# Weights of the second layer converted during the first and kept in DRAM; the exponent moved by two ScalarE passes

## The chip, the cores and the metric

One core of a Trainium2 chip. The metric is the device time of one launch in microseconds, taken as the median over runs. Engines are called by the profile's names: PE (TensorE), DVE (VectorE), ACT (ScalarE), POOL (GpSimd), SP (the queue that issues nearly all DMAs here).

## What is computed

```python
X = np.fft.fft(np.fft.fft(x, axis=1), axis=2)      # x: (2, 3008, 256)
t = X.real.astype(np.float32).reshape(6016, 256)
h = t @ moe_w_in                                   # 256 -> 2048
g = np.where(h >= 1, h, np.where(h <= -1, 0.0, (h + 1) ** 2 / 4))
y = g @ moe_w_out                                  # 2048 -> 256
h = y @ moe2_w_in
return (np.maximum(0.01 * h, h) @ moe2_w_out).astype(np.float32)
```

The four weight matrices are float64, everything else is float32.

## The kernel before

The tokens are cut into eight units of 752, and the 2048 hidden features into sixteen slices of 128. One **step** n is one unit and one slice: 128 steps for the first layer (N1 = 128), 128 for the second, then four more to empty the pipe. The loop over the steps is at line 674. A matrix product keeps nearly float32 precision by splitting each operand into a high part and a low part and adding three products (high·high, high·low, low·high).

**A first-layer step** (`layer_1`, line 624) on PE is `first_1` (6 matmuls into a PSUM pair `p`, of which there are two) and `second` for step n − 4 (12 matmuls into `acc`). In between, DVE makes `aa` (line 635), the two halves of `h` (638, 639) and the maximum (648, for step n − 1); ACT makes two clamped halves (641, 645), the high part `gh` (569, for step n − 2) and a square (652); POOL makes the low part `gl` (573, for step n − 2), which `second` reads two steps later. **A second-layer step** (`layer_2`, line 655) has 24 matmuls, and less work elsewhere: ACT 660 and 569, DVE 661, POOL 573. Each sixteenth step ends with `store` (575), two copies on ACT and two on DVE.

**Weights** arrive as float64 in chunks of 128 x 512 (`w1`, `w2` for the first layer, `w3`, `w4` for the second, eight chunks each), 512 KB a chunk, into a ring of four buffers `rw`. `ToF32` (line 200) turns a chunk into float32 with integer operations on the two 32-bit halves of a float64:

- `begin`: the sign is taken off the high word, by ACT (`Abs`, line 215) or, while `clamping[0]` is set (all first-layer steps), by DVE (line 212);
- `exponent`: DVE clamps (line 219), then shifts and masks (line 221);
- `join`: DVE puts back the sign (line 225) and the last three bits of the mantissa (line 228).

After that a chunk is split into a high part (ACT: 248 or 263) and a low part (DVE: 252 or 267; for `w2` POOL at 267).

**The order of the work** is the program's own: each engine runs its instructions in the order in which they are issued here. Up to the first step, a list (`ORDER`, line 135) gives it; the eight `w1` chunks and `w2` chunks 0 to 3 are converted there. From then on a table `jobs` gives the functions to call at the end of a step. `plan` (599) puts the seven stages of a chunk on seven steps in a row. `w2` chunk j, 4 to 7, starts at step 1 + 3(j − 4), so that its `begin`, `exponent` and `join` fall on steps 3, 4, 5 for the first and 12, 13, 14 for the last. `w3` starts at step 114 and `w4` at step 126 (lines 612 to 617): `plan_late` (603) puts `exponent` and `join` on one step, and the two splits on the next. `split_y` (591) splits the first layer's result of one unit and half: ACT 593, DVE 594; for unit 0 at steps 118 and 121.

Of the kernel before, what the change touches and what calls it, by code (L numbers as in the profile page):

```python
# [9 lines left out]

F32 = mybir.dt.float32
FR = mybir.dt.float32r
I32 = mybir.dt.int32
I64 = mybir.dt.int64
AF = mybir.ActivationFunctionType
ALU = mybir.AluOpType

B, S, D, DFF = 2, 3008, 256, 2048
P = 128
# [107 lines left out]

LEAST = float(np.array(896 << 20, np.uint32).view(np.float32))  # L130
MOST = float(np.array((1151 << 20) - 1, np.uint32).view(np.float32))

ORDER = [s.strip() for s in """
load_w1 1, load_w1 4, load_x 0 0, load_cd, load_x 0 1, load_w1 2, load_x 0 2, w1_begin 1, load_w1 3,
w1_exponent 1, w1_begin 4, w1_join 1, w1_exponent 4, add_x 0 0, load_w1 0, g_product 1, load_me 2, w1_join 4,
# [24 lines left out]
def fnet_moe_kernel(ctx: ExitStack, tc: tile.TileContext, xpq, dft_e, dft_o, dft_d, sgn,  # L162
                    w1, w2, w3, w4, out):
    nc = tc.nc
    PSUM = bass.MemoryType.PSUM

    def pool(n, bufs, stack=ctx, side="left"):
        return stack.enter_context(tc.tile_pool(name=n, bufs=bufs, side=side, reuse_waits="tile"))
# [20 lines left out]
    V, A, G, T = nc.vector, nc.scalar, nc.gpsimd, nc.tensor  # L189
    g128 = sm.tile([P, NF], F32, name="g128")  # L190

    clamping = [False]

    def load_w(w, j):

        t = rw.tile([P, 512], I64, tag="rw", name="rw")
        nc.sync.dma_start(out=t, in_=w[j])
        return t

    class ToF32:  # L200

        def load(self, w, j):
            self.raw = load_w(w, j)

        def begin(self):
            v = self.raw.bitcast(I32).rearrange("p (n w) -> p n w", w=2)
            self.low, self.high = v[:, :, 0], v[:, :, 1]
            self.tmp = cv.tile([P, 512], I32, tag="tw", name="tw")  # L210
            if clamping[0]:
                V.tensor_scalar(out=self.tmp, in0=self.high, scalar1=0x7FFFFFFF, scalar2=None,  # L212
                                op0=ALU.bitwise_and)
            else:
                A.activation(self.tmp.bitcast(F32), self.high.bitcast(F32), AF.Abs)

        def exponent(self):
            t = self.tmp
            V.tensor_scalar(out=t.bitcast(F32), in0=t.bitcast(F32), scalar1=LEAST, scalar2=MOST,  # L219
                            op0=ALU.max, op1=ALU.min)  # L220
            V.tensor_scalar(out=t, in0=t, scalar1=3, scalar2=0x3FFFFFF8,  # L221
                            op0=ALU.logical_shift_left, op1=ALU.bitwise_and)

        def join(self):
            V.scalar_tensor_tensor(out=self.tmp, in0=self.high, scalar=-0x40000000, in1=self.tmp,  # L225
                                   op0=ALU.bitwise_and, op1=ALU.bitwise_or)
            c = cv.tile([P, 512], I32, tag="cw", name="cw")
            V.scalar_tensor_tensor(out=c, in0=self.low, scalar=29, in1=self.tmp,  # L228
                                   op0=ALU.logical_shift_right, op1=ALU.bitwise_or)
            self.f32 = c.bitcast(F32)  # L230

    def new_wa(j, nm):
        return wp.tile([P, 2, 4, P], FR, tag="wa", name=f"{nm}{j}")

    def first_weights(j):

        c = ToF32()
        t = {}

        def views():  # L240
            v = t["w"].rearrange("p q (h e) f -> p q h e f", e=2)
            s = c.f32.rearrange("p (q h f) -> p q h f", q=2, h=2)
            return [(v[:, q, :, 0, :], v[:, q, :, 1, :], s[:, q]) for q in range(2)]

        def high():
            t["w"] = new_wa(j, "wc")
            for hi, _, s in views():
                A.copy(hi, s)

        def low():  # L250
            for hi, lo, s in views():
                V.tensor_tensor(out=lo, in0=s, in1=hi.bitcast(F32), op=ALU.subtract)
            wa[j] = t["w"]

        return [lambda: c.load(w3, j), lambda: None, c.begin, c.exponent, c.join, high, low]

    def second_weights(w, j, nm, engine):
        c = ToF32()
        t = {}

        def high():
            t["w"] = wpb.tile([P, 2, 2, D], FR, tag="wb", name=f"{nm}{j}")
            A.copy(t["w"][:, :, 0, :], c.f32.rearrange("p (q d) -> p q d", q=2))

        def low():
            v = t["w"]
            engine.tensor_tensor(out=v[:, :, 1, :], in0=c.f32.rearrange("p (q d) -> p q d", q=2),  # L267
                                 in1=v[:, :, 0, :].bitcast(F32), op=ALU.subtract)
            wb[j] = v

        return [lambda: c.load(w, j), lambda: None, c.begin, c.exponent, c.join, high, low]

    with tc.manual_schedule():
# [256 lines left out]
        N1 = NU * NF  # L530
# [60 lines left out]
        def split_y(u, d):  # L591
            y = yp[u % 2].tile([P, 2, 2, H4], FR, tag="yh", name=f"yh{u}{d}")
            A.copy(y[:, 0], yt[u][:, d])
            V.tensor_tensor(out=y[:, 1], in0=yt[u][:, d], in1=y[:, 0].bitcast(F32), op=ALU.subtract)
            yh.setdefault(u, {})[d] = y

        jobs = {}

        def plan(step, stages, at=0):
            for i, s in enumerate(stages[at:]):  # L600
                jobs.setdefault(step + i, []).append(s)

        def plan_late(step, st):

            load, _, begin, exponent, join, high, low = st
            plan(step, [load, lambda: None, begin, lambda: (exponent(), join()), lambda: (high(), low())])

        for j in range(4, 8):
            plan(1 + 3 * (j - 4), w2s[j])
        w3s = [first_weights(j) for j in range(8)]  # L610
        w4s = [second_weights(w4, j, "wd", V) for j in range(8)]
        for j in range(8):
            if j < 3:
                plan(N1 - 14 + 3 * j, w3s[j])
            else:
                plan_late(N1 - 4 + 3 * (j - 3), w3s[j])
            plan_late(N1 - 2 + 2 * j, w4s[j])
        for d in range(2):
            plan(N1 - 10 + 3 * d, [lambda d=d: split_y(0, d)])
        for u in range(1, NU):  # L620
            plan(N1 + NF * (u - 1) + 8, [lambda u=u: split_y(u, 0)])
            plan(N1 + NF * (u - 1) + 11, [lambda u=u: split_y(u, 1)])
# [1 line left out]
        def layer_1(n):  # L624

            new = n < N1
            if new:  # L630
                u, f = divmod(n, NF)
                w, o = (378, 1) if u % 4 == 0 else (H4, 0)
                p = first_1(u, f)
                aa = ta.tile([P, 378], F32, tag="aa", name="aa")
                V.scalar_tensor_tensor(out=aa[:, :w], in0=ct[u][:, :w], scalar=g128[:, f:f + 1],  # L635
                                       in1=p[:, 0, :w], op0=ALU.mult, op1=ALU.add)
                hp[n] = h = th.tile([P, 2, H4], F32, tag="h", name="h")
                V.tensor_tensor(out=h[:, 0], in0=aa[:, 0:H4], in1=p[:, 1, 0:H4], op=ALU.subtract)  # L638
                V.tensor_tensor(out=h[:, 1], in0=aa[:, o:o + H4], in1=p[:, 1, o:o + H4], op=ALU.add)  # L639
                rp[n] = r = t5.tile([P, 2, H4], F32, tag="r", name="r")  # L640
                A.activation(r[:, 0], h[:, 0], CLAMP, scale=15.5)  # L641
            if 0 <= n - 2 < N1:
                high(n - 2)
            if new:
                A.activation(r[:, 1], h[:, 1], CLAMP, scale=15.5)  # L645
            if 0 <= n - 1 < N1:
                gp[n - 1] = g = rp.pop(n - 1)
                V.tensor_tensor(out=g, in0=hp.pop(n - 1), in1=g, op=ALU.max)  # L648
            if 0 <= n - 2 < N1:
                low(n - 2)  # L650
            if new:
                A.activation(r, r, AF.Square, scale=0.5 / 15.5, bias=0.5)  # L652
                sums(n)
# [18 lines left out]
                    store(m, m < N1)  # L672

        for n in range(2 * N1 + LAG):
            clamping[0] = n < N1
            if n < N1:
                layer_1(n)
            else:
                if n < N1 + 2:
                    layer_1(n)  # L680
                if n == N1 + 1:
                    only1.close()
                    right.close()
# [53 lines left out]
```

## Time and profile before

| | us |
|---|---|
| median of 3 runs | 1064.48 (1064.13 to 1065.47) |
| the profiled execution, its own time | 1063.04 |
| its span, first to last instruction | 1061.3 |
| PE busy | 1013.8 (96%) |
| DVE busy | 643.9 (61%) |
| ACT busy | 603.1 (57%) |
| POOL busy | 489.0 (46%) |

Busy times are sums over a program whose stages differ: the transform and the first weights up to about 90 us, the first layer's steps to about 510, the second layer's after that. PE's busy share is an upper bound, since its matmuls overlap. A row of the timeline gives start, duration, engine, line, operation and tiles, then in brackets how long the engine sat idle before it and what released it.

### The profile page before, as it was taken

How to read it: one execution, taken by the hardware profiler on the slowest of the kernel's cores; microseconds unless marked ns; L12 is line 12 of the kernel's file. 1: busy time of each engine (PE TensorE's matmuls, PEld its weight loads, DVE VectorE, ACT ScalarE, POOL GpSimd, SP SyncE). 2: the span in 40 equal slices, each digit the busy share in tenths (PEclk: the TensorE clock that was granted, in tenths of full speed). 3: DMA queues.
4: the chain of work that ended last, by engine and by line, in shares of the span. 5: the costliest groups of instructions: out<-in, count | busy, mean ns of one | idle time of the engine just before them, and what ended most of it. 6: DMA issues, size and time to landing. Idle time of an engine off the chain costs nothing.

```text
span 1061.3 us, 14375 instructions
## 1 busy us (share of the span) xinstructions
PE 1013.8 (96%) x5656; PEld 977.8 (92%) x5656; DVE 643.9 (61%) x952; ACT 603.1 (57%) x934; POOL 489.0 (46%) x274
## 2 busy tenths in 40 slices
PE   7996779999999999997898999999999999999998
PEld 6656779999999999997897999999999999999998
DVE  5988998878787878799999523232322323223221
ACT  2347568888888888875764444444444444444433
POOL 1014565656555655544443444444444444444443
PEclk9898999999999999999999999999999999999999
DMA  9921110000000000000131000000000000000000
GB/s 299 337 64 40 40 40 2 1 1 1 1 1 1 1 1 2 1 21 23 58 99 41 30 1 1 30 1 30 1 1 30 1 30 1 1 30 1 30 1 30
DMA packets 9859, 35.04 MB, mean 33 GB/s; under 512 B 1216, under 2 KB 1216, under 8 KB 9536
## 3 DMA queue, kind: packets, MB, share of 16 engines
q1 hardware_dynamic: 8928, 30.98, 8.0%
q0 software_dynamic: 864, 3.15, 1.6%
q8 instruction: 44, 0.72, 0.3%
q14 instruction: 23, 0.19, 0.1%
HBM read 27.96 MB, written 6.16 MB: 32 GB/s over the span
## 4 chain that ended last, share of the span: by engine, by line
PE 77%; DVE 15%; DMA 3%; issue 2%; ACT 2%; POOL 0%; SPq 0%; DVEq 0%; POOLq 0%; ACTq 0%
PE acc L564 43%; PE q L551 23%; PE p L540 10%; DVE cw L228 2%; DVE r L648 2%; DMA rw<-in_w_dram 2%; DVE tw L221 2%; DVE tw L219 1%; DVE tw L225 1%; DVE aa L635 1%; DVE h L639 1%; DMA x<-in_xpq_dram 1%; DVE h L638 1%; DVE s L661 1%; DVE tw L212 1%
## 5 line engine op out<-in xcount | busy, mean ns | idle before, releaser
L573 POOL TENSOR_TENSOR gl<-s,gh 128x752 fp32r<-128x752 f32 x128 | 234.3, 1830 | 297.7 <-ACT gh L569 297.7
L573 POOL TENSOR_TENSOR gl<-r,gh 128x752 fp32r<-128x752 f32 x128 | 236.8, 1850 | 195.6 <-ACT gh L569 171.9
L661 DVE TENSOR_TENSOR s<-q,s 128x752 f32<-128x752 f32 x128 | 120.2, 939 | 298.3 <-ACT s L660 298.3
L551 PE MATMUL q<-yh,wc 128*128 128x376 f32 x1536 | 287.6, 336 | 8.6 <-DVE s L661 8.6
L564 PE MATMUL acc<-gh,wb 128*128 128x376 f32 x1024 | 283.5, 338 | 1.6 <-POOL wb L267 1.3
L564 PE MATMUL acc<-gh,wd 128*128 128x376 f32 x1024 | 278.6, 333 | 0.0
L551 PEld LDWEIGHTS q<-yh,wc 128*128 128x128 f32 x1536 | 267.3, 190 | 10.8 <-DVE s L661 7.2
L569 ACT CAST gh<-s 128x752 fp32r<-128x752 f32 x128 | 105.1, 821 | 161.2 <-PE acc L564 152.3
L564 PEld LDWEIGHTS acc<-gh,wb 128*128 128x128 f32 x1024 | 188.5, 190 | 5.0 <-ACT r L645 2.3
L564 PE MATMUL acc<-gl,wb 128*128 128x376 f32 x512 | 173.6, 339 | 16.8 <-POOL gl L573 16.7
L564 PEld LDWEIGHTS acc<-gh,wd 128*128 128x128 f32 x1024 | 186.1, 188 | 0.1
L660 ACT ACTIVATE s<-q 128x752 f32<-128x752 f32 x128 | 102.2, 799 | 126.1 <-PE q L551 126.0
L564 PE MATMUL acc<-gl,wd 128*128 128x376 f32 x512 | 170.5, 333 | 0.0
L540 PE MATMUL p<-bt,wa 127*128 127x376 f32 (+3 forms) x768 | 156.8, 340 | 9.3 <-DVE h L639 6.1
L540 PEld LDWEIGHTS p<-bt,wa 128*128 128x128 f32 (+1 forms) x768 | 136.2, 191 | 13.0 <-issue 4.7
L648 DVE TENSOR_TENSOR r<-h,r 128x752 f32<-128x752 f32 x128 | 122.7, 958 | 3.5 <-ACT r L652 3.5
L641 ACT ACTIVATE r<-h 128x376 f32<-128x376 f32 x128 | 66.4, 519 | 97.5 <-DVE h L638 86.6
L564 PEld LDWEIGHTS acc<-gl,wb 128*128 128x128 f32 x512 | 97.4, 190 | 21.8 <-POOL gl L573 21.8
L635 DVE SCALAR_TENSOR_TENSOR aa<-ct,g,p 128x376 f32<-128x376 f32 (+1 forms) x128 | 77.3, 604 | 56.7 <-PE p L540 56.6
L652 ACT ACTIVATE r<-r 128x752 f32<-128x752 f32 x128 | 106.8, 834 | 4.1
L569 ACT CAST gh<-r 128x752 fp32r<-128x752 f32 x128 | 103.2, 806 | 0.2 <-DVE r L648 0.2
L564 PEld LDWEIGHTS acc<-gl,wd 128*128 128x128 f32 x512 | 96.1, 188 | 0.0
(71 smaller groups left out, 661.0 us busy)
## 6 DMA issues: line engine op xcount, KB each, us to landing
rw<-in_w_dram SPq DMA_DIRECT2D x32, 512.0 KB, 3.5
out_dram<-o SPq DMA_DIRECT2D x16, 376.0 KB, 2.4
x<-in_xpq_dram SPq DMA_DIRECT2D x6, 512.0 KB, 6.7
x<-in_xpq_dram POOLq DMA_DIRECT2D x6, 512.0 KB, 7.5
me<-in_dft_e_dram SPq DMA_DIRECT2D x4, 567.0 KB, 16.6
mo<-in_dft_o_dram SPq DMA_DIRECT2D x2, 1128.0 KB, 20.3
cd<-in_dft_d_dram SPq DMA_DIRECT2D x1, 256.0 KB, 6.1
sg<-in_sgn_dram SPq DMA_DIRECT2D x1, 1.0 KB, 6.2
```

Of the source, the lines that this page charges most:

```text
L221: V.tensor_scalar(out=t, in0=t, scalar1=3, scalar2=0x3FFFFFF8, op0=ALU.logical_shift_left, op1=ALU.bitwise_and)
L540: T.matmul(p[:, j, :n], lhsT=w[:m, 2 * j + x, :], rhs=b[:m, 2 * j + y, :n], start=(a == 0), stop=(a == 2))
L551: T.matmul(p[:, t, :H4], lhsT=w[:, 2 * d + x, :], rhs=y[d][:, z, t, :], start=(a == 0), stop=(a == 5))
L564: T.matmul(acc[k][:, :H4], lhsT=w[:, x, m * P:(m + 1) * P], rhs=y[:, t, :], start=(f == 0 and i == 0), stop=(f == NF - 1 and i == 2))
L569: A.copy(gh[n], gp[n])
L573: G.tensor_tensor(out=gl[n], in0=gp.pop(n), in1=gh[n].bitcast(F32), op=ALU.subtract)
L635: V.scalar_tensor_tensor(out=aa[:, :w], in0=ct[u][:, :w], scalar=g128[:, f:f + 1], in1=p[:, 0, :w], op0=ALU.mult, op1=ALU.add)
L641: A.activation(r[:, 0], h[:, 0], CLAMP, scale=15.5)
L648: V.tensor_tensor(out=g, in0=hp.pop(n - 1), in1=g, op=ALU.max)
L652: A.activation(r, r, AF.Square, scale=0.5 / 15.5, bias=0.5)
L660: A.activation(g, p, AF.Copy, scale=0.01)
L661: V.tensor_tensor(out=g, in0=p, in1=g, op=ALU.max)
```

## The change

- **Conversion** (`ToF32`): `begin` is now two ACT passes, everywhere: one multiplies the high word, read as float32, by 2^-9 and holds it within ±240, the other multiplies by 2^-103 in place. Together they lower the exponent by 112. The DVE clamp and the DVE way of taking off the sign are gone; `exponent` is one DVE pass, and `join` is cut into `sign` and `rest`.
- **`w3`**: chunk j is loaded at step 20 + 12j, `begin` comes 2 steps later, `exponent` 3, `sign` 6, and `rest` 9, with a DMA that writes the float32 chunk (256 KB) to a DRAM scratch. At step 122 + 2j it is read back into an `rw` buffer, and three steps later split into `wc`.
- **`w4`**: loaded at step 125 + 2j, `begin` and `exponent` 2 steps later, `join` 3, both splits 4.
- **`split_y`** of unit 0 moves from steps 118 and 121 to 102 and 108.

```diff
+from concourse.act_funcs import IDENTITY_SAT240 as HOLD
...
+    sp = ctx.enter_context(tc.tile_pool(name="sp", bufs=1, space=bass.MemoryType.DRAM))
...
-            if clamping[0]:
-                V.tensor_scalar(out=self.tmp, in0=self.high, scalar1=0x7FFFFFFF, scalar2=None,
-                                op0=ALU.bitwise_and)
-            else:
-                A.activation(self.tmp.bitcast(F32), self.high.bitcast(F32), AF.Abs)
+            t = self.tmp.bitcast(F32)
+            A.activation(t, self.high.bitcast(F32), HOLD, scale=2.0 ** -9)
+            A.activation(t, t, AF.Copy, scale=2.0 ** -103)
...
-            V.tensor_scalar(out=t.bitcast(F32), in0=t.bitcast(F32), scalar1=LEAST, scalar2=MOST,
-                            op0=ALU.max, op1=ALU.min)
-            V.tensor_scalar(out=t, in0=t, scalar1=3, scalar2=0x3FFFFFF8,
+            V.tensor_scalar(out=self.tmp, in0=self.tmp, scalar1=3, scalar2=0x7FFFFFF8,
                             op0=ALU.logical_shift_left, op1=ALU.bitwise_and)
...
+        def spill():
+            c.rest()
+            t["dram"] = sp.tile([P, 512], F32, name=f"w3f{j}")
+            nc.sync.dma_start(out=t["dram"], in_=c.f32)
+
+        def load():
+            t["f32"] = rw.tile([P, 512], I64, tag="rw", name="rf").bitcast(F32)[:, :512]
+            nc.sync.dma_start(out=t["f32"], in_=t["dram"])
...
-        return [lambda: c.load(w3, j), lambda: None, c.begin, c.exponent, c.join, high, low]
+        return [lambda: c.load(w3, j), c.begin, c.exponent, c.sign, spill, load, high, low]
...
-            if j < 3:
-                plan(N1 - 14 + 3 * j, w3s[j])
-            else:
-                plan_late(N1 - 4 + 3 * (j - 3), w3s[j])
-            plan_late(N1 - 2 + 2 * j, w4s[j])
+            plan_at(20 + 12 * j, *zip((0, 2, 3, 6, 9), w3s[j]))
+            plan_at(N1 - 6 + 2 * j, *zip((0, 3, 3), w3s[j][5:]))
+            plan_at(N1 - 3 + 2 * j, *zip((0, 1, 2, 2, 3, 4, 4), w4s[j]))
         for d in range(2):
-            plan(N1 - 10 + 3 * d, [lambda d=d: split_y(0, d)])
+            plan_at(N1 - 26 + 6 * d, (0, lambda d=d: split_y(0, d)))
...
-            clamping[0] = n < N1
```

`plan_at(step, (offset, stage), ...)` puts each stage on the step at its offset.

## Rows read from the trace of the kernel before

**Rows 1.** Part 1 of the page: busy time, share of the span, instructions.

```profile
PE 1013.8 (96%) x5656; PEld 977.8 (92%) x5656; DVE 643.9 (61%) x952; ACT 603.1 (57%) x934; POOL 489.0 (46%) x274
```

**Rows 2.** Busy time by stretch: PE, PEld, DVE, ACT, POOL; then clock, DMA, GB/s.

```profile
100.00:120.00 20.00, 16.06 (x89) 14.84 (x88) 19.69 (x25) 10.83 (x18) 10.61 (x6) 1.00 0.08 26
...
300.00:400.00 100.00, 99.90 (x578) 99.02 (x577) 80.41 (x133) 80.94 (x134) 58.31 (x32) 1.00 0.00 1
...
700.00:800.00 100.00, 100.00 (x585) 100.00 (x584) 29.08 (x29) 42.33 (x54) 44.19 (x25) 1.00 0.02 9
```

**Rows 3.** Timeline of a first-layer step without conversion, around 301 to 308.

```profile
301.39 0.61 DVE L635 SCALAR_TENSOR_TENSOR aa<-ct,g,p 128x378 f32<-128x378 f32 x1 [0.61 <-PE p L540]
...
302.95 0.93 DVE L648 TENSOR_TENSOR r<-h,r 128x752 f32<-128x752 f32 x1
...
303.09 0.81 ACT L569 CAST gh<-r 128x752 fp32r<-128x752 f32 x1
...
304.03 1.81 POOL L573 TENSOR_TENSOR gl<-r,gh 128x752 fp32r<-128x752 f32 x1 [1.29 <-ACT gh L569]
...
304.35 0.84 ACT L652 ACTIVATE r<-r 128x752 f32<-128x752 f32 x1
...
307.56 0.33 PE L564 MATMUL acc<-gl,wb 128*128 128x376 f32 x1
```

**Rows 4.** Timeline of steps 3 to 15, where `w2` chunks 4 to 7 are converted.

```profile
92.18 0.60 DVE L635 SCALAR_TENSOR_TENSOR aa<-ct,g,p 128x378 f32<-128x378 f32 x1
...
94.84 2.02 DVE L212 TENSOR_SCALAR tw<-rw 128x512 int32<-128x512 int32 x1
...
99.18 0.42 DVE L219 TENSOR_SCALAR tw<-tw 128x512 f32<-128x512 f32 x1
99.63 1.92 DVE L221 TENSOR_SCALAR tw<-tw 128x512 int32<-128x512 int32 x1
...
103.88 0.69 DVE L225 SCALAR_TENSOR_TENSOR tw<-rw,tw 128x512 int32<-128x512 int32 x1
...
104.11 2.10 POOL L573 TENSOR_TENSOR gl<-r,gh 128x752 fp32r<-128x752 f32 x1 [2.84 <-ACT gh L569]
...
104.67 2.09 DVE L228 SCALAR_TENSOR_TENSOR cw<-rw,tw 128x512 int32<-128x512 int32 x1
...
145.01 0.60 DVE L635 SCALAR_TENSOR_TENSOR aa<-ct,g,p 128x378 f32<-128x378 f32 x1
```

**Rows 5.** PE's timeline from step 117 to step 144, across the change of layer.

```profile
462.93 1.19 PE L540 MATMUL p<-bt,wa 128*128 128x376 f32 x6
...
504.52 1.30 PE L540 MATMUL p<-bt,wa 128*128 128x376 f32 x6
...
509.31 2.22 PE L551 MATMUL q<-yh,wc 128*128 128x376 f32 x12
...
578.55 3.91 PE L551 MATMUL q<-yh,wc 128*128 128x376 f32 x12 [2.94 <-DVE s L661]
...
588.46 2.21 PE L551 MATMUL q<-yh,wc 128*128 128x376 f32 x12
```

**Rows 6.** ACT's groups by line and shape: count, busy us, mean ns, idle before.

```profile
L215 ACT ACTIVATE tw<-rw 128x512 f32<-128x512 f32 x24 | 15.9, 674 | 13.4 <-DMA rw<-in_w_dram 13.2
L248 ACT CAST wc<-cw 128x256 fp32r<-128x256 f32 x16 | 5.7, 401 | 6.3 <-DVE cw L228 6.3
...
L263 ACT CAST wd<-cw 128x512 fp32r<-128x512 f32 x8 | 4.9, 618 | 3.9 <-DVE cw L228 3.8
```

**Rows 7.** ACT's timeline: two `begin` passes, and two of the three table loads.

```profile
66.93 1.50 ACT L215 ACTIVATE tw<-rw 128x512 f32<-128x512 f32 x2
...
85.80 1.28 ACT L641 ACT_TABLE_LOAD   x1
...
515.80 1.28 ACT L215 ACT_TABLE_LOAD   x1
```

**Rows 8.** DMA issues: count, KB each, median us from issue to landing.

```profile
rw<-in_w_dram SPq DMA_DIRECT2D x32, 512.0 KB, 3.5
```

More of the change, by code (lines that the diff above doesn't have):

```diff
@@ L126, in _token_rows @@
     return np.concatenate(rows)
-LEAST = float(np.array(896 << 20, np.uint32).view(np.float32))
-MOST = float(np.array((1151 << 20) - 1, np.uint32).view(np.float32))
 ORDER = [s.strip() for s in """
@@ L190, in fnet_moe_kernel @@
     g128 = sm.tile([P, NF], F32, name="g128")
-    clamping = [False]
     def load_w(w, j):
@@ L210, in begin, with sign, rest @@
             self.tmp = cv.tile([P, 512], I32, tag="tw", name="tw")
-            if clamping[0]:
-                V.tensor_scalar(out=self.tmp, in0=self.high, scalar1=0x7FFFFFFF, scalar2=None,
-                                op0=ALU.bitwise_and)
-            else:
-                A.activation(self.tmp.bitcast(F32), self.high.bitcast(F32), AF.Abs)
+            t = self.tmp.bitcast(F32)
+            A.activation(t, self.high.bitcast(F32), HOLD, scale=2.0 ** -9)
+            A.activation(t, t, AF.Copy, scale=2.0 ** -103)
         def exponent(self):
-            t = self.tmp
-            V.tensor_scalar(out=t.bitcast(F32), in0=t.bitcast(F32), scalar1=LEAST, scalar2=MOST,
-                            op0=ALU.max, op1=ALU.min)
-            V.tensor_scalar(out=t, in0=t, scalar1=3, scalar2=0x3FFFFFF8,
+            V.tensor_scalar(out=self.tmp, in0=self.tmp, scalar1=3, scalar2=0x7FFFFFF8,
                             op0=ALU.logical_shift_left, op1=ALU.bitwise_and)
-        def join(self):
-            V.scalar_tensor_tensor(out=self.tmp, in0=self.high, scalar=-0x40000000, in1=self.tmp,
+        def sign(self):
+            V.scalar_tensor_tensor(out=self.tmp, in0=self.high, scalar=-0x80000000, in1=self.tmp,
                                    op0=ALU.bitwise_and, op1=ALU.bitwise_or)
+        def rest(self):
             c = cv.tile([P, 512], I32, tag="cw", name="cw")
@@ L230, in join @@
             self.f32 = c.bitcast(F32)
+        def join(self):
+            self.sign()
+            self.rest()
     def new_wa(j, nm):
@@ L238, in first_weights @@
         t = {}
+        def spill():
[5 more added lines that the diff above has]
+            nc.sync.dma_start(out=t["f32"], in_=t["dram"])
         def views():
             v = t["w"].rearrange("p q (h e) f -> p q h e f", e=2)
-            s = c.f32.rearrange("p (q h f) -> p q h f", q=2, h=2)
+            s = t["f32"].rearrange("p (q h f) -> p q h f", q=2, h=2)
             return [(v[:, q, :, 0, :], v[:, q, :, 1, :], s[:, q]) for q in range(2)]
@@ L601, in plan, with plan_at @@
                 jobs.setdefault(step + i, []).append(s)
-        def plan_late(step, st):
-            load, _, begin, exponent, join, high, low = st
-            plan(step, [load, lambda: None, begin, lambda: (exponent(), join()), lambda: (high(), low())])
+        def plan_at(step, *stages):
+            for at, s in stages:
+                jobs.setdefault(step + at, []).append(s)
         for j in range(4, 8):
```

## The prediction

> **What bounds the kernel now.** I read the busy shares first: PE is busy for 96% of the span, DVE for 61% [rows 1]. That average says little, so the second view is the busy time by stretch [rows 2]. From 300 to 400 us PE is full: 578 matmuls in 100 us, 18 a step, so a first-layer step takes 3.11 us. From 700 to 800 it is full too: 585 matmuls, 24 a step, 4.10 us. From 100 to 120 PE is busy for 16.06 of 20 us, and DVE for 19.69: there DVE sets the pace. PE's timeline shows a second such stretch. It starts steps 117 and 128 at 462.93 and 509.31, 46.4 us for eleven steps that cost 34.2 at 3.11 us; steps 128 and 144 start at 509.31 and 588.46, 79.2 us for sixteen that cost 65.6 [rows 5]. That is 12.2 + 13.6 = **25.8 us lost around the change of layer**. In the first stretch DVE starts steps 3 and 15 at 92.18 and 145.01, 52.8 us for twelve that cost 37.3 [rows 4]: **15.5 us lost early**. Both are the stretches with weight conversion; the rest of the steps runs at PE's pace.
>
> Third, the timeline of one step, to see how much room there is. Without conversion DVE idles 0.61 us a step before `aa`, waiting for PE [rows 3]. `gl`, the last link of a step's chain, starts at 304.03 and takes 1.81; PE wants it at 307.56 [rows 3]. So the chain has **1.7 us of slack**: something that delays DVE or ACT once by less costs nothing, and some 0.6 us a step is won back.
>
> Last, why conversion is so dear for DVE. `L219` takes 0.42, and `L221` behind it 1.92; `L225` takes 0.69, and the like-sized `L228` behind it 2.09 [rows 4]. POOL's `gl` (104.11, 2.10) stands between [rows 4]: the first pass behind `L648` gets through, the second is held until POOL is done. A held pass costs about 1.4 us more, and each step has one POOL instruction to be held by.
>
> **Part 1, the early stretch.** Per chunk the change takes away `L212` (2.02 at the first chunk, which was held; taken as 0.42, like `L219`, for three more) and puts one pass in the place of `L219` and `L221` [rows 4]. The one that stays is first behind `L648`, so it costs what `L219` does, 0.42, and not 2.3: 1.9 saved. `join` stays at 0.69 + 2.09. Sum: 4 x 1.9 + 2.0 + 3 x 0.4 = 10.8 us, **taken as 11**. ACT gets two passes a chunk, each bounded by 0.67 [rows 6]; in three steps it has 3 x 2.5 us of its own (80.94 us in 100 [rows 2]), plus 1.35 and one split of 0.62 [rows 6], 9.5 us. DVE needs (52.8 - 10.8)/4 = 10.5. So ACT hides the passes; if DVE got faster than that, ACT would be next. The lower bound is 8, if the single `exponent` pass is held at half of the chunks (4 x 1.4 / 2 = 2.8 less). The upper is 15.5, all of the loss, should `rest` no longer be held because ACT, and so `gl`, runs later.
>
> The Trainium skill speaks against moving a multiplication this way: ScalarE: Activation LUTs, section "Rules for kernel authors", gives mul, max and min to VectorE, as the faster engine per element. The rows bear the rule out for one pass alone (0.67 on ACT, 0.42 on DVE). By it the four chunks would lose 0.25 us a pass, and this term would be near -2 in place of 11; but the pass that goes was a held one, and on the engine that is full.
>
> **Part 2, the change of layer.** `w3`'s conversion leaves it altogether: per `w3` chunk DVE keeps only the low split, per `w4` chunk it loses the clamp. For the second layer's steps count two at a time, one chunk of each kind, against 8.2 us of PE. DVE's own work is 29.08/24.4 = 1.2 us a step [rows 2], 2.4. `exponent` 0.42, `sign` and `rest` 0.69 each [rows 4], the low splits of `w4` and `w3` (two inputs, 512 elements a row each, so `L225`'s 0.69 each) make 3.2. That is 5.6 without holds, and 8.4 with one hold of 1.4 a step. The same count for before has five chunks in six steps, each 0.42 + 0.42 + 3 x 0.69 = 2.9: 14.5 + 7.2 + 6 x 1.4 = 30.1 us, where the rows give 79.2 x 6/16 = 29.7, so the count can be trusted. After, it gives 0 to 0.2 us lost per two steps, 0 to 2 for sixteen steps. ACT has (42.33/24.4) x 2 = 3.5 of its own [rows 2], plus 1.35 + 0.62 + 0.80 [rows 6] = 6.3 of 8.2: hidden.
>
> Two new waits stand in DVE's queue: `exponent` of `w4` is issued on the step of its own `begin`, and both low splits on that of their high splits, so DVE stands still until ACT gets there, with the next step's `aa` or `L661` behind it, and PE behind that. At step 125 this can be priced: `L648` ends at 303.9, ACT's square at 305.2, then a high split of 0.40 [rows 3, 6]; POOL holds until 305.84; the two lows end near 306.6, where `aa` should have started at 304.5. That is 2.1 late against 1.7 of slack: 0.4 lost. At step 127 ACT's two passes and a further split come on top, but PE then has the second layer's first twelve matmuls, which need neither; taken as 0.5, bound 3. In the second layer `p` or `q` has two buffers, and DVE frees one well ahead. **Sum: 25.8 - 1.8 = 24 us**, bounds 19 (the waits cost all of 3, the holds 4) and 25.8.
>
> The reloads: SP issues 16 more DMAs (8 writes, 8 reads, 256 KB), and the DMA engines have nothing else then. 512 KB land in 3.5 us [rows 8]; a reload has three steps, over 9 us, less the time it waits for an `rw` buffer, freed a step before. Hidden. If it came later than about 8 us, ACT would stop in front of its high split, and `gh` of the step behind it.
>
> **Part 3, the steady first layer** gets what has left: per `w3` chunk two ACT passes on one step (1.35 against some 0.6 of idle time: 0.75 late, within the slack), and three DVE passes on three steps, 0.42, 0.69, 0.69 against 0.61 each [rows 3, 4], all first behind `L648`; POOL's `gl` is then held for up to 0.6, within the slack. The write stands in SP's queue behind `rest`, with only the next load behind it, three steps later. That is nothing per chunk while each delay stays below 1.7. The two `split_y` (steps 102, 108) are different: DVE waits for ACT's copy, as at step 125, about 2.1 late: 0.4 each. **Cost taken as 1 us**; from 0 to 3.
>
> **Part 4, before the first step.** Twelve chunks get one more ACT pass (at most 0.67) and one DVE pass less (0.42); in a chain of one chunk this is 0.25 longer, on a busy DVE 0.42 shorter. The last place where it counts is 66.93, two `begin`s together [rows 7]: the chain to 85.80 gets about 0.5 longer there. Table loads: `Abs` and the clamp of line 641 need a load between them in both directions (85.80 and 515.80, 1.28 each [rows 7]), the copies and squares none. The load at 515.80 goes, which lies in the stretch counted in part 2. That at 85.80 is on the chain; no row tells if HOLD's table has the clamp. **Taken as 0**, from 1.5 gained (load gone) to 1.5 lost.
>
> **The sum.** 11 + 24 - 1 + 0 = 34 us. Against the profiled execution's own 1063.0 that is 1029.0; the median of the runs is 1.4 above it, so 1030.
>
> **The rivals.**
> - *The waits for ACT keep DVE the bound in the change of layer* (chance 0.12). One more hold and 0.4 of waiting for every two steps, 10.2 against 8.2, so 2.0 x 8 = 16 less part 2's allowance of 2: 14 lost. For: both waits are new, and the count with holds already fills 8.2. Against: one POOL instruction a step can hold only once. 1044.
> - *The spread work is not free* (0.10). If each `w3` chunk loses one hold beyond slack, 8 x 1.4 = 11: 1041. For: DVE and ACT are 80% busy there [rows 2]. Against: every DVE pass stands first.
> - *HOLD and the clamp are in different tables* (0.04). Two loads of 1.28 for each of twelve chunks. Early, ACT's 9.5 becomes 12.1 in three steps against DVE's 10.5, 4 x 1.6 = 6 lost; in the middle 1.35 + 2.56 is 3.3 late, 1.6 over the slack, x 8 = 13. 1049. The Trainium skill's page ScalarE activation tables: per-element evaluation and per-set limits, section "What a function is on this engine", puts functions of different sets one load of 1283 ns apart; the rows' 1.28 agrees.
> - *Slower* (0.05): nothing of a chunk's work fits the first layer. Held at every pass, a chunk costs 0.42 + 2 x 0.69 + 3 x 1.4 = 6.0 us of DVE; if PE lost all of it, 8 x 6.0 = 48 in place of 1: 1077. It decides from 35/8 = 4.4 us a chunk. Against: 0.61 us of idle time in each of twelve steps, 7.3 us a chunk.
>
> **How the numbers follow.** The forecast has 0.67, the four rivals 0.31, no change 0.02. Its own bounds are 1063.0 + 1.4 less (15.5 + 25.8 - 0 + 1.5 = 42.8) and less (8 + 19 - 3 - 1.5 = 22.5): 1022 to 1042. The range goes up to 1044, which takes in the first two rivals. A measurement here can tell about 0.2% (2 us) from no change. Faster 0.93, same 0.02, slower 0.05.
>
> **What would show it.** Right: from 100 to 150 us PE at 90% or more, where it was 80%; from 460 to 590 PE with no waits for DVE over 1 us; from 160 to 450 the same step of 3.11; two table loads; `L661` in the second layer with idle time before it from the start. Wrong: a gap of PE at each `w3` chunk, twelve steps apart; loads in pairs; ACT waiting for the reload.

## The result, and the profile after

| | before | after |
|---|---|---|
| median, us | 1064.97 (1064.13 to 1066.04) | **1040.8** (1040.43 to 1042.03) |
| profiled execution, us | 1063.04 | 1040.43 |
| its span, us | 1061.3 | 1038.7 |

The ratio is 0.9774, 95% interval 0.9758 to 0.9791. The span is 22.6 us shorter; the forecast had 34. So the direction was right and the size a third short. The starts of four steps on PE cut that difference up:

| stretch (starts on PE) | before, us | after, us | gained | forecast |
|---|---|---|---|---|
| up to step 4 | 91.56 | 91.62 | -0.1 | 0 |
| step 4 to 19 (`w2` chunks 4 to 7) | 64.66 | 63.00 | **1.7** | 11 |
| step 19 to 117 (steady first layer) | 306.71 | 310.41 | **-3.7** | -1 |
| step 117 to 128 | 46.38 | 34.22 | 12.2 | } 24 |
| step 128 to 144 | 79.15 | 66.61 | 12.5 | } |

Part 1 of the page of after, against [rows 1]: DVE has lost 24 us of work, ACT has gained 21.

```profile
PE 1004.1 (97%) x5656; PEld 971.7 (94%) x5656; DVE 619.7 (60%) x912; ACT 624.1 (60%) x973; POOL 495.6 (48%) x274
```

Busy time by stretch of after; the columns are those of [rows 2].

```profile
100.00:120.00 20.00, 17.87 (x99) 16.57 (x98) 18.91 (x23) 12.68 (x23) 10.74 (x7) 1.00 0.07 26
120.00:140.00 20.00, 15.10 (x81) 13.33 (x80) 18.08 (x25) 15.64 (x27) 12.20 (x7) 1.00 0.00 1
140.00:160.00 20.00, 16.54 (x90) 14.96 (x89) 19.15 (x26) 13.58 (x24) 14.30 (x8) 1.00 0.01 1
300.00:400.00 100.00, 99.53 (x575) 98.50 (x574) 86.55 (x140) 83.56 (x138) 60.20 (x32) 1.00 0.07 25
...
520.00:540.00 20.00, 20.00 (x119) 20.00 (x117) 18.01 (x20) 13.69 (x22) 9.34 (x5) 1.00 0.29 94
540.00:560.00 20.00, 20.00 (x118) 20.00 (x118) 18.81 (x22) 13.77 (x24) 9.12 (x6) 1.00 0.15 53
```

From 520 on PE is full although DVE is busy for 18 of 20 us: the work now fits. From 100 to 160 PE is busy for 49.5 of 60 us. Something there is still late, and it isn't DVE's busy time alone, which has fallen (56.1 of 60 us, 58.5 before).

**The early stretch.** The timeline of after, DVE and POOL, over one period of three steps from `aa` to `aa`, in order of time.

```profile
103.77 0.59 DVE L641 SCALAR_TENSOR_TENSOR aa<-ct,g,p 128x378 f32<-128x378 f32 x1
...
106.17 0.60 DVE L641 SCALAR_TENSOR_TENSOR aa<-ct,g,p 128x378 f32<-128x378 f32 x1
...
106.40 1.81 POOL L581 TENSOR_TENSOR gl<-r,gh 128x752 fp32r<-128x752 f32 x1 [3.11 <-ACT gh L577]
...
107.73 1.28 DVE L654 TENSOR_TENSOR r<-h,r 128x752 f32<-128x752 f32 x1
...
109.33 0.43 DVE L213 TENSOR_SCALAR tw<-tw 128x512 int32<-128x512 int32 x1 [0.32 <-ACT tw L210]
...
110.55 1.80 POOL L581 TENSOR_TENSOR gl<-r,gh 128x752 fp32r<-128x752 f32 x1 [2.33 <-issue]
...
111.80 1.35 DVE L654 TENSOR_TENSOR r<-h,r 128x752 f32<-128x752 f32 x1 [0.49 <-ACT r L658]
...
112.31 1.99 POOL L275 TENSOR_TENSOR wb<-cw,wb 128x512 fp32r<-128x512 f32 x1
...
113.07 1.78 DVE L217 SCALAR_TENSOR_TENSOR tw<-rw,tw 128x512 int32<-128x512 int32 x1
...
114.26 2.27 POOL L581 TENSOR_TENSOR gl<-r,gh 128x752 fp32r<-128x752 f32 x1
...
114.88 2.21 DVE L222 SCALAR_TENSOR_TENSOR cw<-rw,tw 128x512 int32<-128x512 int32 x1
...
117.01 0.60 DVE L641 SCALAR_TENSOR_TENSOR aa<-ct,g,p 128x378 f32<-128x378 f32 x1
```

The same two steps in the timeline of before: there the low split of `w2` (`L267`) begins 0.3 us before the held pass `L221` ends, and runs on beside `aa` and `h`.

```profile
112.23 1.81 POOL L573 TENSOR_TENSOR gl<-r,gh 128x752 fp32r<-128x752 f32 x1 [1.07 <-issue]
...
112.33 2.00 DVE L221 TENSOR_SCALAR tw<-tw 128x512 int32<-128x512 int32 x1
...
114.01 1.49 POOL L267 TENSOR_TENSOR wb<-cw,wb 128x512 fp32r<-128x512 f32 x1
...
116.65 0.69 DVE L225 SCALAR_TENSOR_TENSOR tw<-rw,tw 128x512 int32<-128x512 int32 x1
...
116.89 2.13 POOL L573 TENSOR_TENSOR gl<-r,gh 128x752 fp32r<-128x752 f32 x1 [1.40 <-ACT gh L569]
...
117.37 2.19 DVE L228 SCALAR_TENSOR_TENSOR cw<-rw,tw 128x512 int32<-128x512 int32 x1
```

Before, the period is 106.68 to 119.49 (the first of these ends the held `L228` of [rows 4]), 12.8 us; after, 13.24. Two passes fewer save 0.85 and the hold on `L221` is gone (1.5), but `sign` is now held at 1.78 in place of 0.69 (1.1), the maximum `L654` lies under `gl` on two steps (1.28 and 1.35 for 0.94; 0.75), and DVE waits twice for ACT (0.32 + 0.49 = 0.81). That is some 2.7 against 2.4: a period isn't shorter but longer, by 0.4. The 1.7 us come from the first chunk alone, whose `L212` had been held [rows 4]: `aa` of step 6 starts at 103.77 in place of 106.68, 2.9 earlier, and three periods give 1.3 of it back.

**The steady first layer.** Nearly every step takes 3.11, also those with a pass of a `w3` chunk. The loss sits in six steps: 36 and 84 (3.99 and 4.04, where a step with a store took 3.47 to 3.50 before), 105 and 111 (3.84, 3.88), 113 (4.23) and, by 0.05, 116. DVE's timeline of after at its steps 35, 102 and 110 shows one cause each: a held `exponent` behind a store, a wait of `split_y` for ACT, a held `sign`.

```profile
208.38 0.99 DVE L593 COPY y<-acc 128x376 f32<-128x376 f32 x2
209.29 1.93 DVE L213 TENSOR_SCALAR tw<-tw 128x512 int32<-128x512 int32 x1
...
421.22 0.94 DVE L602 TENSOR_TENSOR yh<-y,yh 128x752 fp32r<-128x752 f32 x1 [2.04 <-ACT yh L601]
...
446.59 2.30 DVE L217 SCALAR_TENSOR_TENSOR tw<-rw,tw 128x512 int32<-128x512 int32 x1
```

**The change of layer.** PE's timeline of after, the starts of steps 117, 128, 132 and 133, against [rows 5].

```profile
465.03 1.22 PE L548 MATMUL p<-bt,wa 128*128 128x376 f32 x6
...
499.25 2.22 PE L559 MATMUL q<-yh,wc 128*128 128x376 f32 x12
...
515.68 2.21 PE L559 MATMUL q<-yh,wc 128*128 128x376 f32 x12
518.48 0.44 PE L572 MATMUL acc<-gh,wd 128*128 128x376 f32 x1 [0.58 <-DVE y L593]
520.65 2.21 PE L559 MATMUL q<-yh,wc 128*128 128x376 f32 x12
```

Steps 117 to 128 take 34.22, PE's own 11 x 3.11; of the 16 that follow only step 132 is long (4.97, at a store). The table of DMA issues has the scratch: 2.2 us to write a chunk, 2.6 to read it back, and no row of ACT waits for a read.

```profile
rw<-in_w_dram SPq DMA_DIRECT2D x32, 512.0 KB, 3.7
...
w3f<-cw SPq DMA_DIRECT2D x8, 256.0 KB, 2.2
rf<-w3f SPq DMA_DIRECT2D x8, 256.0 KB, 2.6
```

### The profile page after: what moved, and what is told of

Its sections match the earlier page's. It is cut to its first block, busy times and chain, and to the rows that moved or that the text cites. A ratio compares the mean times of both kernels' runs of the same rounds, so it can differ in the third digit from the quotient of the medians.

```text
span 1038.7 us, 14411 instructions
## 1 busy us (share of the span) xinstructions
PE 1004.1 (97%) x5656; PEld 971.7 (94%) x5656; DVE 619.7 (60%) x912; ACT 624.1 (60%) x973; POOL 495.6 (48%) x274
## 4 chain that ended last, share of the span: by engine, by line
PE 78%; DVE 9%; ACT 7%; issue 3%; DMA 2%; POOL 0%; DVEq 0%; ACTq 0%; POOLq 0%; SPq 0%
PE acc L572 43%; PE q L559 24%; PE p L548 9%; DVE r L654 2%; ACT gh L577 2%; DMA rw<-in_w_dram 2%; ACT r L658 1%; DVE cw L222 1%; DVE tw L217 1%; DVE aa L641 1%; ACT r L647 1%; DVE h L644 1%; ACT r L651 1%; PE do L442 1%; DMA x<-in_xpq_dram 1%
## 5 line engine op out<-in xcount | busy, mean ns | idle before, releaser
L581 POOL TENSOR_TENSOR gl<-r,gh 128x752 fp32r<-128x752 f32 x128 | 242.4, 1895 | 175.9 <-ACT gh L577 135.3
L667 DVE TENSOR_TENSOR s<-q,s 128x752 f32<-128x752 f32 x128 | 120.2, 939 | 301.4 <-ACT s L666 301.2
L559 PE MATMUL q<-yh,wc 128*128 128x376 f32 x1536 | 283.8, 333 | 0.0
L548 PEld LDWEIGHTS p<-bt,wa 128*128 128x128 f32 (+1 forms) x768 | 136.5, 191 | 10.5 <-issue 5.0
L654 DVE TENSOR_TENSOR r<-h,r 128x752 f32<-128x752 f32 x128 | 129.3, 1010 | 4.5 <-ACT r L658 4.4
```

What stands on the lines that cost most here:

```text
L548: T.matmul(p[:, j, :n], lhsT=w[:m, 2 * j + x, :], rhs=b[:m, 2 * j + y, :n], start=(a == 0), stop=(a == 2))
L559: T.matmul(p[:, t, :H4], lhsT=w[:, 2 * d + x, :], rhs=y[d][:, z, t, :], start=(a == 0), stop=(a == 5))
L667: V.tensor_tensor(out=g, in0=p, in1=g, op=ALU.max)
```

## The experiments

Each kernel differs from the changed one by the edit shown, unless said otherwise; nothing of the computation is left out in any. Times are medians, ratios go to the kernel before with their 95% interval, and the columns are PE's stretches of the table above, each from the one profiled execution. The kernels with the new conversion are the same program up to the first steps, and yet start step 4 between 91.5 and 93.4 us; the whole carries that spread, the stretches don't.

| run | us | ratio | 4 to 19 | 19 to 117 | 117 to 128 | 128 to 144 |
|---|---|---|---|---|---|---|
| after | 1040.8 | 0.9774 [0.9758, 0.9791] | 63.0 | 310.4 | 34.2 | 66.6 |
| conversion alone | 1052.5 | 0.9884 [0.9869, 0.9900] | 63.4 | 306.7 | 42.6 | 72.7 |
| schedule alone | 1048.2 | 0.9855 [0.9835, 0.9875] | 64.7 | 312.6 | 34.2 | 69.9 |
| POOL's low split later | 1046.3 | 0.9831 [0.9815, 0.9847] | 67.2 | 311.3 | 34.2 | 66.6 |
| ACT's passes earlier | 1038.5 | 0.9763 [0.9744, 0.9781] | 61.3 | 310.4 | 34.2 | 66.6 |
| one DVE pass a step | 1033.8 | 0.9714 [0.9700, 0.9729] | 54.7 | 310.4 | 34.2 | 66.6 |
| that, ACT's passes earlier | 1031.2 | 0.9694 [0.9679, 0.9708] | 52.0 | 310.4 | 34.2 | 66.6 |
| middle moved | 1037.7 | 0.9751 [0.9735, 0.9768] | 63.2 | 306.8 | 34.2 | 66.6 |
| last two together | **1027.0** | 0.9654 [0.9640, 0.9669] | 53.3 | 306.9 | 34.2 | 66.6 |
| low split on DVE | 1036.5 | 0.9738 [0.9721, 0.9754] | 58.7 | 310.5 | 34.2 | 66.6 |
| last two together, low split on DVE | 1029.0 | 0.9669 [0.9649, 0.9688] | 54.5 | 307.0 | 34.2 | 66.6 |

**Which half of the change pays where.** First the new conversion in the kernel before, with the old order of the chunks; then the new order and the scratch with the old conversion.

```diff
 # before, new conversion only
...
+            A.activation(t, self.high.bitcast(F32), HOLD, scale=2.0 ** -9)
+            A.activation(t, t, AF.Copy, scale=2.0 ** -103)
...
```

> The conversion of the changed kernel (two ScalarE passes, one exponent pass) in the order of the kernel before: w3 is converted around the change of layer, no scratch. The two parts of the change are told apart. My count of DVE passes says: around the change of layer five chunks in six steps need 5 x (0.42 + 3 x 0.69) + 7.2 + 6 x 1.4 = 28.1 us against 24.6 of PE, so that of the 25.8 us lost there some 14 to 18 stay; with 1.8 us gained before step 19, as in the changed kernel, the whole is 10 to 13 us faster than before, 1052 to 1055. Rival: the holds by POOL, not the number of passes, set DVE's pace, and one hold comes back for each one taken away; then nearly all of the 25.8 us stays and the whole is within 5 us of before.

```diff
 # after, old conversion
-            A.activation(t, self.high.bitcast(F32), HOLD, scale=2.0 ** -9)
-            A.activation(t, t, AF.Copy, scale=2.0 ** -103)
+            if clamping[0]:
+                V.tensor_scalar(out=self.tmp, in0=self.high, scalar1=0x7FFFFFFF, ...)
...
+            clamping[0] = n < N1
```

> The conversion of the kernel before (five DVE passes in the first layer, Abs on ScalarE in the second) in the order of the changed kernel, with the scratch. If moving w3 is what gave the 24.7 us around the change of layer, this keeps about 20 of them (one clamp more per w4 chunk and a table load of 1.28 us are back) and loses in the steady first layer, where the exponent step now has two passes, the second held (0.42 + 1.92 against 0.61 of idle time, 1.7 late, about all of the slack): 0 to 1 us a chunk on top of the 3.9 us measured in the changed kernel. Early stretch as before. Whole: 1044 to 1054. Rival: the two ScalarE passes are needed as much as the order; then at least half of the gain is gone, 1054 or more.

Steps 117 to 128 reach PE's own 34.2 with the schedule alone, and 42.6 with the conversion alone: the new order is what frees that stretch. It takes `w3` out of it and moves `split_y`; the two were not run apart. In the steady first layer the old conversion costs 2.2 us more than the new one (312.6 against 310.4). In steps 128 to 144 the schedule brings 9.3 us (79.15 to 69.85), and the conversion 3.2 more. Early, only the conversion counts, and the period of after is there already with the old schedule: from 104.44 to 117.67, 13.23 us, in DVE's timeline of that run.

```profile
104.44 0.60 DVE L631 SCALAR_TENSOR_TENSOR aa<-ct,g,p 128x378 f32<-128x378 f32 x1
...
113.73 1.78 DVE L221 SCALAR_TENSOR_TENSOR tw<-rw,tw 128x512 int32<-128x512 int32 x1
115.55 2.20 DVE L224 SCALAR_TENSOR_TENSOR cw<-rw,tw 128x512 int32<-128x512 int32 x1
117.67 0.60 DVE L631 SCALAR_TENSOR_TENSOR aa<-ct,g,p 128x378 f32<-128x378 f32 x1
```

So the lost early gain is the conversion's own doing, and neither the scratch nor the moved chunks have a part in it.

**What holds `sign`?** The first theory took POOL's low split, which stands right in front of `gl` at 112.31. It was moved one step later. The rival was that DVE waits for ACT; to try it, ACT's two passes were moved one step earlier.

```diff
 # low split later
-            plan(1 + 3 * (j - 4), w2s[j])
+            plan_at(1 + 3 * (j - 4), *zip((0, 1, 2, 3, 4, 5, 7), w2s[j]))
```

> The changed kernel with the low half of w2 chunks 4 to 7 on POOL one step later. Theory A (why the early stretch gained 1.8 us and not 11): the hold that went with the clamp comes back at the sign pass, because POOL's low half of the chunk before stands right before gl on the step of the sign pass (1.78 us in place of 0.69). Then the sign pass is short again here, 0.7 us, and the stretch from step 4 to step 19 on PE, 63.0 us in the changed kernel, is 2 to 4 us shorter: 59 to 61. Rival B: ScalarE is late, with a high half and two passes on one step, and DVE waits for it; then nothing changes (62.5 to 63.5). Whole: A 1037 to 1039, B 1040 to 1041.

```diff
 # ACT's passes earlier
-            plan(1 + 3 * (j - 4), w2s[j])
+            plan_at(1 + 3 * (j - 4), *zip((0, 0, 1, 3, 4, 5, 6), w2s[j]))
```

> The changed kernel with the two ScalarE passes of w2 chunks 4 to 7 one step earlier, so that they no longer share a step with the high half of the chunk before. Rival B: the 0.3 us that the exponent pass waits for ScalarE and the 0.5 us that the maximum waits go, 0.8 us a chunk, so the stretch from step 4 to step 19 is 2 to 3 us shorter than 63.0. Theory A: these waits are filled by holds, less than 1 us changes. Whole: B 1037.5 to 1039, A 1040 to 1041.

With the low split later the period stays at 13.25 (104.52 to 117.78), and the holds only change hands. The timeline of that run, DVE and POOL:

```profile
113.70 1.90 POOL L581 TENSOR_TENSOR gl<-r,gh 128x752 fp32r<-128x752 f32 x1 [0.59 <-POOL gl L581]
...
113.83 2.32 DVE L217 SCALAR_TENSOR_TENSOR tw<-rw,tw 128x512 int32<-128x512 int32 x1
...
115.56 1.74 POOL L275 TENSOR_TENSOR wb<-cw,wb 128x512 fp32r<-128x512 f32 x1
...
116.18 1.67 DVE L222 SCALAR_TENSOR_TENSOR cw<-rw,tw 128x512 int32<-128x512 int32 x1
```

Now `gl` holds `sign` and the low split holds `rest`. As stated the theory fell: taking the low split from that place frees nothing, as POOL's next instruction moves up into it. The whole became 5.5 us slower, mostly because the last chunk's weights now come too late: PE waits 3.79 us for `wb` at step 18 (1.35 in after). With ACT's passes earlier, its two waits go and the period falls to 12.03, 1.2 less; `sign` and `rest` stay at 1.78 and 2.20. The gain of 1.7 us over the stretch is less than three such periods, since the first chunk loses: with its `begin` on step 2 the maximum of step 4 waits 0.70 for ACT, and the `exponent` behind it falls under `gl` (98.39, 2.03 us in place of 0.41), so that the first full period begins at 105.56 in place of 103.77. The waits are real, but the smaller part.

**One DVE pass a step.** If what counts is that two passes stand on one step, putting `sign` and `rest` on two steps should free one of them, without a pass less.

```diff
-        return [lambda: c.load(w, j), lambda: None, c.begin, c.exponent, c.join, high, low]
+        return [lambda: c.load(w, j), lambda: None, c.begin, c.exponent, c.join, high, low, c.sign, c.rest]
...
-            plan(1 + 3 * (j - 4), w2s[j])
+            plan_at(1 + 3 * (j - 4),
+                    *zip((0, 2, 3, 4, 5, 5, 6), (w2s[j][i] for i in (0, 2, 3, 7, 8, 5, 6))))
```

> The changed kernel with sign and rest of w2 chunks 4 to 7 on steps of their own (chunk offsets: exponent 3, sign 4, rest 5; high and low as before at 5 and 6). Theory A': a DVE pass is held if it is not the first behind the maximum, so with three passes on three steps nothing or little is held; the early stretch from step 4 to step 19, 63.0 us in the changed kernel, falls by the two holds of the join step, 1.1 + 1.4 us, for three or four chunks, to 53 to 56, and the whole to 1031 to 1034. Rival: POOL is late by then and holds the first pass of a step as well, one hold for one, so that the stretch stays at 60 or more and the whole at 1038 or more.

The second kernel moves `begin` of chunks 5 to 7 one step earlier as well (offsets `(0, 1 + (j == 4), 3, 4, 5, 5, 6)`).

> As the run before (passes on steps of their own), and the two ScalarE passes of chunks 5 to 7 one step earlier, so that they don't share a step with a high half. By the run with only the earlier passes ScalarE's lateness costs about 1.2 us a chunk: the stretch from step 4 to step 19 is 2 to 4 us shorter than in the run before, 50 to 53, near PE's own 46.7; whole 1028 to 1032. If ScalarE is hidden once DVE has less to do, the same within 1 us as the run before.

Steps 4 to 19 fall from 63.0 to 54.7, and to 52.0 with the earlier `begin`. The timeline of the second of the two, DVE and POOL:

```profile
108.11 0.42 DVE L213 TENSOR_SCALAR tw<-tw 128x512 int32<-128x512 int32 x1
...
108.50 1.82 POOL L581 TENSOR_TENSOR gl<-r,gh 128x752 fp32r<-128x752 f32 x1 [1.10 <-issue]
...
110.29 1.99 POOL L275 TENSOR_TENSOR wb<-cw,wb 128x512 fp32r<-128x512 f32 x1
...
111.05 1.78 DVE L217 SCALAR_TENSOR_TENSOR tw<-rw,tw 128x512 int32<-128x512 int32 x1
...
115.24 0.68 DVE L222 SCALAR_TENSOR_TENSOR cw<-rw,tw 128x512 int32<-128x512 int32 x1
...
115.38 2.21 POOL L581 TENSOR_TENSOR gl<-r,gh 128x752 fp32r<-128x752 f32 x1 [0.86 <-DVE r L654]
```

`exponent` and `rest` begin before that step's `gl` and cost 0.42 and 0.68. `sign` alone begins inside a POOL instruction, the low split, and is held. The low splits of two chunks start 10.07 us apart (110.29 and 120.36), where PE's own three steps take 9.3. Of the 5.3 us that 52.0 still has over PE's own 46.7, step 4 has 2.4: there PE, after 4.2 us of waiting for DVE, runs at a granted clock of 0.50 (92 to 96 us), the level of 1.2 GHz. Step 18 has 1.7, where PE waits for POOL's last low split.

**The middle.** The load of each `w3` chunk one step earlier, so that `exponent` no longer meets the store; and `split_y` cut into its ACT half on one step and its DVE half on the next.

```diff
-            plan_at(20 + 12 * j, *zip((0, 2, 3, 6, 9), w3s[j]))
+            plan_at(19 + 12 * j, *zip((0, 2, 3, 6, 9), w3s[j]))
...
-            plan_at(N1 - 26 + 6 * d, (0, lambda d=d: split_y(0, d)))
+            plan_at(N1 - 26 + 5 * d, (0, lambda d=d: split_high(0, d)), (1, lambda d=d: split_low(0, d)))
```

> The changed kernel with the w3 chunks one step earlier, so that no DVE pass falls on a step with the copies of the store, and split_y of unit 0 with its ScalarE half one step ahead of its DVE half (steps 102 and 103, 107 and 108). The 3.9 us that the steady first layer lost (steps 36, 84, 105, 111 and 113 took 0.5 to 1.1 us more) should be gone but for 0 to 1 us: step 19 to 117 in 306.6 to 307.6 us, against 310.4; whole 1037 to 1038. If instead the passes cost as such, spread over all chunks, nothing or less than 1 us is gained.

Steps 19 to 117 take 306.8, against 306.7 before the change: the whole loss of the middle was these meetings. A `w3` chunk costs nothing by itself.

**All of it.** Both edits, the spread passes with the earlier `begin` and the moved middle:

> The three edits of the runs before together (passes of w2 on steps of their own, ScalarE passes earlier, the middle freed of coincidences). They lie in different stretches, so the gains add: 1026 to 1030, if the passes alone on a step are not held; 1034 to 1037 if they are.

At 1027.0 it is faster than both kernels, and its interval lies clear of that of the change. The gains nearly add up: of the 11.0 us by which the spread kernel shortens steps 4 to 19, 9.7 are there, and 3.5 of the middle's 3.6. One hold accounts for the 1.3 us that are missing. `sign` of the first chunk is alone on its step and first behind the maximum in both kernels; in the spread kernel with the earlier `begin` it started at 101.94, 0.01 before `gl`, and took 0.68. Here it starts 0.08 behind `gl` and takes 2.31, as the timeline of DVE and POOL shows:

```profile
101.65 1.83 POOL L581 TENSOR_TENSOR gl<-r,gh 128x752 fp32r<-128x752 f32 x1 [0.64 <-POOL gl L581]
...
101.73 2.31 DVE L217 SCALAR_TENSOR_TENSOR tw<-rw,tw 128x512 int32<-128x512 int32 x1
```

**Is the low split the last holder?** It goes to DVE, once in the changed kernel and once in the fastest one.

```diff
-        w2s = [second_weights(w2, j, "wb", G) for j in range(8)]
+        w2s = [second_weights(w2, j, "wb", G if j < 4 else V) for j in range(8)]
```

> The changed kernel with the low split of `w2` chunks 4 to 7 on DVE in place of POOL (nothing left out). Theory A: POOL's 2.0 us low split is what holds the first of DVE's two passes on a step; without it `sign` costs 0.69 in place of 1.78, DVE pays 0.69 for the low split, and at most one further hold on the step where the low split and the next chunk's `exponent` now stand together: steps 4 to 19 take 63.0 - 4 x 0.4 = 61 to 62 us, the whole 1039 to 1040. Theory B: a hold is not tied to the low split; whatever second pass stands on a step is held by `gl`, so the new pair (low split, `exponent`) gives one hold of 1.4 a chunk while `sign` goes free: 63 to 66 us, the whole 1040 to 1044.

> The fastest kernel so far (passes spread over steps, earlier ACT passes, middle steps moved; 1027.0 us, 53.3 us for steps 4 to 19) with the low split of `w2` chunks 4 to 7 on DVE in place of POOL (nothing left out). There `sign` alone is still held (1.78). Theory A (POOL's low split holds it): `sign` falls to 0.69, the low split costs 0.69 on DVE: 51.5 to 53 us for steps 4 to 19, the whole 1025 to 1027. Theory B (the second of two passes on one step is held): the low split and the next `exponent` stand on one step, one of them is held at about 1.9: 54 to 58 us, the whole 1028 to 1032.

Neither theory's range held the first: 58.7 us for steps 4 to 19 where the ranges began at 61. A held `sign` stays (2.32, under `gl`), but `rest` behind it is now free (0.69), since POOL has only one instruction on that step; and the new pair, low split and `exponent`, costs 0.68 + 0.41, for `gl` comes late there. Besides, step 18 no longer waits for POOL (3.11 in place of 4.71). In the fastest kernel `sign` is free at last, and the hold turns up at `exponent`, which now stands second. The timeline there, DVE and POOL:

```profile
107.81 0.68 DVE L275 TENSOR_TENSOR wb<-cw,wb 128x512 fp32r<-128x512 f32 x1
...
108.19 1.98 POOL L581 TENSOR_TENSOR gl<-r,gh 128x752 fp32r<-128x752 f32 x1 [1.10 <-ACT gh L577]
...
108.41 2.04 DVE L213 TENSOR_SCALAR tw<-tw 128x512 int32<-128x512 int32 x1
...
112.78 0.68 DVE L217 SCALAR_TENSOR_TENSOR tw<-rw,tw 128x512 int32<-128x512 int32 x1
```

That is theory B, shown by the rows. The period goes from 10.09 to 11.36. The times say less: the stretch took 54.5 in place of 53.3, but step 18 no longer waits for POOL here either, `sign` of the first chunk was free, and step 4 took 6.12 in place of 5.07 (granted clock from 96 to 98 us 0.59 in place of 0.98). In the whole the two kernels' intervals overlap, so which is faster isn't settled by time.

## Why the prediction was right and where it failed

**Part 2, the change of layer: right, in size and in reason.** 24.7 us were gained for 24 forecast. Of the 25.8 lost before, 1.0 is left, 0.87 of it in step 132. The waits for ACT were there, 2.20 us for `exponent` on step 127, 1.63 for the low split on step 125, and up to 1.12 before `L275` later, and PE never felt them; the 0.4 + 0.5 set aside for steps 125 and 127 were not needed. The count of holds came out too: from 528.20 to 536.43 two steps of DVE take 8.23, with two held passes (2.33 and 1.92) and 0.64 of waiting, against PE's 8.2. The first rival, which had DVE as the bound there, is out, if narrowly. The schedule's run shows the reason: without `w3` and `split_y` in the stretch 117 to 128 nothing is lost even with the old, dearer conversion.

**Part 1, the early stretch: the term that failed, 1.7 for 11.** Three steps of the working were wrong.

- *"`join` stays at 0.69 + 2.09."* For three of the four chunks it became 1.78 + 2.21 (or 2.1); only the first kept 0.68 + 2.12. The count of POOL's instructions was wrong: "each step has one POOL instruction to be held by", `gl`. On one step in three POOL has a second one, the low split of `w2`. Before, it ran, but for its first 0.3 us, beside `aa` and `h`, which are not held (0.60 and 0.55 throughout), so the rows around the held passes didn't show it. A step shortened by 1.9 us puts `sign` where it runs. The hold taken from `exponent` was not removed; it moved to the next pass in the queue.
- *"So ACT hides the passes."* The sums over three steps, 9.5 against 10.5, were right and beside the point: the two passes, 0.67 + 0.63, stand on the step that also has the high split's 0.60 and ACT's own 2.6 (two halves, `gh`, the square), 4.5 us in all. DVE without its wait would have been through that step in 3.2 (106.17 to 109.68, less 0.32). It waited 0.32 for `exponent` and 0.49 for the square.
- *"the first pass behind `L648` gets through"*. `sign` is the first pass behind the maximum on its step, and is held: what counts is whether an instruction of POOL is already running. The maximum can be held too. On a step without a pass DVE runs on in 2.40, faster than PE's 3.11, and its next maximum then falls under `gl` (1.28 for 0.94). Being ahead costs 0.34 itself.

The price of a hold, 1.4, was right (1.1 to 1.6), and so, it turns out, was the worth of what the change set free: with the passes spread the same conversion brings 10.0 us over the kernel before in this stretch (64.66 to 54.65), and 12.7 with the earlier `begin`, within the bounds of 8 to 15.5. What failed was where the holds go. That the total of 1040.8 still lies inside the prediction's own bounds of 1022 to 1042 is luck: this term (1.7, bounds 8 to 15.5) and part 3's (3.7 lost, bounds 0 to 3) lie outside theirs, and part 2 near the top of its bounds makes up for it.

**Part 3, the middle: right for a chunk, short for the meetings.** "Nothing per chunk" holds, and the rival by which the spread work is not free, whose total of 1041 is next to the measured one, is out by its mechanism: the chunks that meet nothing cost nothing. `split_y` cost 0.75 for each of the two, not 0.4: behind the first one `gl` comes 2.27 us late (5.38 behind the one before it, where a step has 3.11), a little more than the 2.1 reckoned, PE waits 0.46 for it, and the step gets 0.73 longer. The rate at which a delay is won back was right on the whole: DVE's next three steps take 2.41, 2.77 and 2.56, or 0.70, 0.34 and 0.55 less than PE's. Two costs were not seen at all: `exponent` on the step of a store (steps 35 and 83; 0.5 each over a plain store step), where it is second behind the store's copies, and the held `sign` of the last chunk, two steps behind the second `split_y` (1.1). Both are the early stretch's rule again.

**Part 4, before the first step: right.** The loss is 0.1 us, less than the spread of this stretch over the kernels. The load of tables at 85.80 stays (85.87 in after), that at 515.80 [rows 7] has gone, and no further one came. So a load still stands between the first HOLD and the first clamp, but from 85.87 on both run without another; the rival by which each chunk pays two loads is out. ACT's groups of after have just these two:

```profile
L209 ACT ACT_TABLE_LOAD x1 | 1.3, 1283 | 0.7 <-PEq L727 0.7
...
L647 ACT ACT_TABLE_LOAD x1 | 1.3, 1283 | 0.0
```

Of the signs named beforehand, those of the change of layer came (no wait of PE for DVE over 1 us from 460 to 590, ACT not waiting for a reload), the two loads too, and steps of 3.11 in the middle but for the six. PE at 90% from 100 to 150 did not come (82%), and `L667` in the second layer has no idle time before it at first: what DVE has left there it spends waiting before `L275`.

The rule of the Trainium skill that was weighed against the change (ScalarE: Activation LUTs, section "Rules for kernel authors": mul, max and min to VectorE) would have made the early term -2; 1.7 was measured, 10.0 with the passes spread. Here the two passes on ACT, 1.30 us of busy time, cost 1.2 a period where they met the high split on a step, and the DVE passes and the hold that they replaced had cost 2.4.

## What to carry to other kernels

A hold between two engines is a matter of place, not a property of the instruction that shows it: before taking away a held pass, list every instruction of the other engine in the period and ask which pass will stand beside it afterwards. Give each step one pass that can be held and put it first; here that alone took 8.3 us out of fifteen steps without removing an instruction. First is not enough by itself: `sign` was still held where an instruction of POOL was already running, once one that had begun only 0.08 us before. A sum of busy time over a period shows that an engine has room, not that it has it on the step that needs it.

## What the runs showed of the hardware

- **A held DVE pass does nearly all its work after the POOL instruction is done.** `sign` ends at 113.07 + 1.78 = 114.85, 0.55 after POOL's low split (112.31 + 1.99 = 114.30), and `rest` at 117.09, 0.56 after `gl` (116.53); free, they take 0.69. `exponent` in the last experiment ends at 110.45, 0.28 after `gl` (110.17); free, it takes 0.42. So the price of a hold is what is left of POOL's instruction when the pass starts, less 0.14 in all three. `h`, which takes one of its inputs from PSUM, was not seen held (0.54 to 0.55 throughout, though 252 of its 256 in after begin while POOL is busy); the maximum `L654`, with both inputs in SBUF, takes 0.93 to 2.26.
- **POOL pays as well.** The low split ends some 1.15 us after the DVE pass that is running when it begins: in before that is `L221`, which ends at 114.33, so that it takes 1.49; in after it is the maximum that `gl` held, which ends at 113.15, so that it takes 1.99. `gl` takes 1.80 alone, and 2.27 where `sign` is still running when it begins: it ends 1.68 after `sign`.
- The Trainium skill, SBUF — State Buffer, section "Who interferes with whom", describes the pair of ports that VectorE and GpSimd share as a lock that whoever issues first keeps for a whole instruction. The rows agree in both directions, as far as POOL's spans can be trusted: DVE waits to POOL's end, and a POOL instruction that begins while such a DVE pass is running is longer by most of what is left of that pass.
- 256 KB to a DRAM scratch took 2.2 us from issue to landing, and 2.6 back.
